# Pooled attention with a feed-forward layer: weight splits on ScalarE and VectorE, and K and V loaded one step sooner

## Chip, core and metric

The kernel runs on one core of one Trainium2 chip. The metric is the device time of one execution in microseconds. Its engines are TensorE (PE, with PEld for its weight loads), VectorE (DVE), ScalarE (ACT), GpSimd (POOL) and SyncE (SP), whose queue issues nearly all DMAs here.

## What is computed

Attention over 4 batches x 8 heads, with the 1152 queries of a head averaged in pairs to 576, and then a feed-forward layer with a residual on the 512-wide result:

```python
q_pool = q.reshape(B, H, S // 2, 2, D).mean(axis=3)          # (4, 8, 576, 64)
scores = matmul(q_pool, k.transpose(0, 1, 3, 2)) / sqrt(D)   # (4, 8, 576, 1152)
attn = exp(scores - max(scores))
attn = attn / (sum(attn) + 1e-09)
x = matmul(attn, v)                                          # heads side by side: (4, 576, 512)
xn = (x - mean(x)) / sqrt(var(x) + 1e-06) * g_ln
out = x + maximum(xn @ w_ch1, 0) @ w_ch2                     # 512 -> 2048 -> 512
```

All inputs and outputs are float32. The kernel keeps float32 accuracy with fp16 matmuls by splitting an operand into a high and a low fp16 part: high = fp16(x), low = fp16(x - high).

## The kernel before

Two heads of a batch make a pair; there are 16 pairs (0 to 15), four for each batch. A pair is worked off in 9 steps of 128 pooled query rows, so there are 144 steps, written here as pair.step or as one number i = 9 x pair + step. The order of all work is written out by hand: `step(i)` issues everything of step i, and each engine runs what it gets in that order.

In step i TensorE computes the scores of step i+1 (`emit_s`, lines 390 and 398) into one of two slots of three PSUM banks. VectorE takes the scores of step i and writes them to SBUF with the row's bound (`emit_max`, line 410), ScalarE makes the exponential (line 417) and its high fp16 part (`emit_hi`, line 428). The low part (`emit_lo`) follows in step i+1: on VectorE (line 437), or, for steps 2, 5 and 8 of a pair, on GpSimd (two instructions, lines 239 and 435). Then SP issues a DMA transpose of both parts (line 440). Four steps after its scores, the product with V runs on TensorE (`emit_pv`, line 480); VectorE and ScalarE evacuate it (lines 528, 529 and 540). The PSUM place of that product lies in the slot that the scores use, so a later step's score matmul of line 398 waits until line 540 has read it. The first batch (steps 0 to 35) does without the DMA transpose and transposes on TensorE in float32.

Besides, each pair needs its inputs. `load` fetches K with two DMAs (lines 117 and 118) and V with one (line 121) into one buffer each, `load_q` fetches q (line 129). `bound` (line 182) reads K, q and V on ScalarE for a bound of their size; from these `scales_reduce`, three steps into the pair before, finds scales over TensorE and VectorE. `prep_k` and `prep_q` transpose K and q on TensorE (lines 285, 289, 312, 321) and split them on ScalarE and VectorE (lines 274 and 271), one unit a step, in the order of the table `PREPS`. `take_v` scales and splits V on GpSimd (lines 239 and 266) in two halves, at steps 5 and 7.

When all heads of a block of rows are done, the block is normalized and its feed-forward work goes into a queue of units: first layer (line 631, evacuated by lines 644 on ScalarE and 645 on VectorE) and second layer (line 663, evacuated by line 677 on VectorE). `some_units` issues one unit in a step, and two once the steps are over; a unit is issued only when the weights it needs are split, which `w_done` counts.

The weights come as four parts of four pieces (n = 0 to 15, each 128 x 1024). A piece is scaled and split into slot n of `wsl` out of slot n+1: `w_split_a` scales in place, `w_split_b` makes the high part, `w_split_c` the low part, all three on GpSimd (lines 239 and 806). `w_splits` plans them: the first two parts one instruction at a time during the first batch, the last two parts at fixed steps, 40 to 58. `at(i, ...)` puts work at the end of step i, `pre(i, ...)` at its start. The loads of pair p and its bounds are planned in one loop, with i0 the first step of pair p-1:

```python
at(max(i0 - 1, 0), load, p, "k", nc.sync)
at(i0, load, p, "v", nc.sync)
at(i0 + 1, bound, p, "k")
...
at(i0 + 2, bound, p, "v")
```

Of the kernel before, what the change touches and what calls it, by code (L numbers as in the profile page):

```python
# [9 lines left out]
FP32 = mybir.dt.float32  # L10
# [3 lines left out]
ACTF = mybir.ActivationFunctionType  # L14
ALU = mybir.AluOpType
# [9 lines left out]
def tile_pooled_attention_moe(  # L25
# [18 lines left out]
    nc = tc.nc  # L44
# [4 lines left out]
    C = S // 128  # L49
    HP = H // 2  # L50
# [29 lines left out]
    wsl = const.tile([128, 17, 2, 1024], FP16, name="wsl")  # L80
    gsb = const.tile([128, KD], FP32, name="gsb")
    gs1 = const.tile([128, 2, KD], FP32, name="gs1")
# [5 lines left out]
    wscl = const.tile([128, 4], FP32, name="wscl")  # L88
# [55 lines left out]
    def kt_of(p):  # L144
        st = state(p)
        if "kt" not in st:
            x = tr_p.tile([128, 2304], FP16, tag="kt", name="kt")
            st["kt"] = x[:, 0:2048].rearrange("p (a h n) -> p a h n", a=2, h=2)
            st["k8"] = x[:, 2048:2304].rearrange("p (h n) -> p h n", h=2)
        return st["kt"]  # L150
# [9 lines left out]
    def pool_q(p, eng):  # L160
        x = raws[p, "q"]
        eng.tensor_tensor(x[:, :, 0], x[:, :, 0], x[:, :, 1], op=ALU.add)

    def dup_q(p, eng):
        x = raws[p, "q"]
        eng.tensor_copy(x[:, :, 1], x[:, :, 0])
# [71 lines left out]
    def scaled(dst, src, s=1.0):  # L238
        nc.gpsimd.tensor_scalar(dst, src, s, 1.0, op0=ALU.mult, op1=ALU.mult)  # L239
# [98 lines left out]
    def prep_q_first():  # L338
# [17 lines left out]
    PREPS = (  # L356
        ((prep_k, 0), (prep_k, 2), (prep_q, 0), (prep_q, 1), (prep_k, 1), (prep_q, 2)),
        ((prep_k, 0), (prep_k, 2), (prep_q, 0), (prep_k, 1), (prep_q, 2), (prep_q, 1)),
    )


# [2 lines left out]
    def on_pe(i):  # L364

        return 0 <= i < HP * C
# [394 lines left out]
    def w_reduce(part):  # L761
        while fill:
            drip()
        x, m = wtop[:, part], wmax[:, part:part + 1]
        nc.vector.tensor_scalar(x, x, 2.0 ** -112, None, op0=ALU.mult)
        xi = x.bitcast(I32)
        nc.vector.tensor_scalar(xi, xi, 3, None, op0=ALU.logical_shift_left)
        if part % 2 == 0:

            nc.vector.tensor_tensor(  # L770
                x, x, gsb[:, :, None].to_broadcast([128, KD, 2]), op=ALU.mult
            )
        nc.vector.tensor_reduce(m, x, axis=AX.XY, op=ALU.max, apply_absolute_value=True)
        reds.extend(all_max(m, 1, lambda ps: (w_scales(part, ps), w_splits(part))))
# [17 lines left out]
    w_done = [0] * 4  # L792

    def w_split_a(n):
        part, c = divmod(n, 4)
        x = wsl[:, n + 1].rearrange("p a n -> p (a n)").bitcast(FP32)
        s = gs1[:, part // 2, c:c + 1] if part % 2 == 0 else wscl[:, part:part + 1]
        scaled(x, x, s)

    def w_split_b(n):  # L800
        x = wsl[:, n + 1].rearrange("p a n -> p (a n)").bitcast(FP32)
# [2 lines left out]
    def w_split_c(n):  # L804
        x = wsl[:, n + 1].rearrange("p a n -> p (a n)").bitcast(FP32)
        nc.gpsimd.tensor_tensor(wsl[:, n, 1], x, wsl[:, n, 0], op=ALU.subtract)
        w_done[n // 4] += 1


    todo = {}  # L810

    def at(i, fn, *a):
        todo.setdefault(i, []).append((fn, a))
# [3 lines left out]
    def pre(i, fn, *a):  # L817
        early.setdefault(i, []).append((fn, a))
# [3 lines left out]

    for p in range(1, NP):
        i0 = (p - 1) * C
        at(max(i0 - 1, 0), load, p, "k", nc.sync)
        at(i0, load, p, "v", nc.sync)
        at(i0 + 1, bound, p, "k")
        if p == 1:
            pre(0, behind_scales)
            pre(i0 + 1, pool_q, p, nc.gpsimd)  # L830
            at(i0 + 1, dup_q, p, nc.gpsimd)
            at(i0 + 2, bound, p, "q")
        elif on_pe(i0):
            at(i0 - 4, load_q, p, (nc.sync,))
            at(i0 - 1, lambda p=p: calm.appendleft((lambda n: pool_q(p, nc.gpsimd), 0)))
            at(i0, lambda p=p: calm.appendleft((lambda n: dup_q(p, nc.gpsimd), 0)))
            at(i0 + 2, bound, p, "q")
        else:
            early_q = not on_pe(i0 - 6)
            at(i0 - (12 if early_q else 8), load_q, p, (nc.sync,))  # L840
            at(i0 - (6 if early_q else 4), pool_q, p, nc.vector)
            at(i0 - 2, bound, p, "q")
            at(i0 - 1, dup_q, p, nc.gpsimd)
        if not on_pe(p * C):
            at(i0 + 2, bound, p, "v")
        pre(i0 + 3, scales_reduce, p, 0, 2 if on_pe(p * C) else 3)
        for n in range(2):
            if on_pe(p * C):
                at(i0 + (5, 7)[n], gate)
            at(i0 + (5, 7)[n], take_v, p, n)  # L850
        for n, (fn, u) in enumerate(PREPS[p % HP // 2]):
            late = 1 if on_pe(i0) else 0
            pre(i0 + 4 + n + late, lambda fn=fn, p=p, u=u: preps.append((fn, p, u)))

# [14 lines left out]
    def w_splits(part):  # L869
        for n in range(4):  # L870
            if part < 2:
                calm.extend((fn, 4 * part + n) for fn in (w_split_a, w_split_b, w_split_c))
                continue
            i0 = 22 + 9 * part + 5 * n // 2
            for x, fn in ((0, w_split_a), (1, w_split_b), (2, w_split_c)):
                at(i0 + x, fn, 4 * part + n)


    norms, fresh, turns = deque(), deque(), set()
# [198 lines left out]
    with tc.manual_schedule():  # L1078
# [15 lines left out]
        for n in (2, 5):  # L1094
# [14 lines left out]
            out=kt_of(0).rearrange("p a h n -> p (a h n)")[:, 0:C * D],  # L1109
            in_=raws[0, "k"][:, 0, 0:C].rearrange("p c d -> p (c d)"), func=ACTF.Abs,  # L1110
# [68 lines left out]
```

## Time and profile before

| | us |
|---|---|
| median of 3 runs (lowest, highest) | 813.52 (812.06, 813.91) |
| the profiled execution's own time | 813.32 |
| its span | 811.50 |
| TensorE busy | 781.8 (96%) |
| VectorE busy | 598.6 (74%) |
| ScalarE busy | 544.0 (67%) |
| GpSimd busy | 342.5 (42%) |

The busy time of TensorE counts each matmul to its modelled end, and matmuls overlap, so a busy TensorE is not one at its peak. Its granted clock is at full speed over nearly the whole span. Steps take from 2 to 8 us between one start of line 410 and the next, about 4.8 in the mean; the last one ends shortly after 690 us. A wait in brackets behind an instruction is the idle time of its engine before it, with what ended it.

### The profile page before, as it was taken

Reading aid. Unit: us, or ns where it says so; the run is one execution under the profiler, and the core shown is the slowest. Engines: PE = TensorE matmul, PEld = TensorE weight load, DVE = VectorE, ACT = ScalarE, POOL = GpSimd, SP = SyncE. Lnnn points to the kernel's source line nnn. Section 1 sums busy time; section 2 is a strip of 40 time slices with the busy share of each in tenths; the row PEclk is TensorE's granted clock in tenths of the full one; section 3 lists DMA queues with packets and bytes.
Section 4 is the critical chain, followed back from the end, with each engine's and each line's share of the span. In section 5 each row is a group of like instructions: output and inputs, shape, how many; then the busy total and the mean of one; then the engine's idle time right before and its main releaser. Section 6 shows DMA issues by size and latency. Waiting matters only on the chain.

```text
span 811.5 us, 21278 instructions
## 1 busy us (share of the span) xinstructions
PE 781.8 (96%) x8936; PEld 551.8 (68%) x8936; DVE 598.6 (74%) x1179; ACT 544.0 (67%) x789; POOL 342.5 (42%) x342
## 2 busy tenths in 40 slices
PE   8999999989989999989999999999999999999997
PEld 6788887767565656567666665767575757766764
DVE  5899999878898986898687877887786867521221
ACT  5889888777767777787677686877677776211010
POOL 2012333576999862665453535537161532300000
PEclk9999999999999999999999999999999999999999
DMA  9736545025998989896989798987979786401001
GB/s 282 241 107 219 192 135 172 2 72 109 168 181 154 179 167 201 164 213 116 202 143 220 147 212 145 186 163 144 197 135 196 131 145 121 86 1 27 14 1 27
DMA packets 276017, 115.95 MB, mean 143 GB/s; under 512 B 259280, under 2 KB 259280, under 8 KB 275920
## 3 DMA queue, kind: packets, MB, share of 16 engines
q1 hardware_dynamic: 275440, 113.63, 67.9%
q8 instruction: 70, 1.15, 0.6%
q10 hardware_dynamic: 480, 0.95, 0.4%
q14 instruction: 27, 0.22, 0.1%
HBM read 46.14 MB, written 4.72 MB: 63 GB/s over the span
## 4 chain that ended last, share of the span: by engine, by line
PE 63%; DVE 16%; ACT 7%; DMA 6%; issue 4%; SPq 2%; POOL 2%; ACTq 0%; DVEq 0%
PE psum L663 19%; PE psum L631 17%; PE psum L390 7%; PE psum L480 6%; PE psum L471 5%; DVE pe L410 5%; PE psum L447 3%; DVE hl L437 3%; DMA vr<-in_v_dram 2%; PE psum L398 2%; ACT pe L417 2%; SPq L440 2%; DMA kr<-in_k_dram 1%; DMA stage<-in_moe_w_ch_dram 1%; PE psum L321 1%
## 5 line engine op out<-in xcount | busy, mean ns | idle before, releaser
L410 DVE CUSTOM_DVE_ANT_0 pe<-psum,nought,sc 128x1152 f32<-128x1152 f32 x144 | 203.0, 1410 | 25.2 <-PE psum L197 9.7
L417 ACT ACTIVATE pe<-pe,nb 128x1152 f32<-128x1152 f32 x144 | 180.4, 1253 | 32.4 <-DVE nb L410 31.2
L663 PE MATMUL psum<-wsl,ht 128*128 128x512 f16 x864 | 196.6, 379 | 2.5 <-DVE ht L645 2.1
L631 PEld LDWEIGHTS <-wsl 128*128 128x128 f16 x1920 | 169.6, 98 | 25.3 <-issue 7.6
L631 PE MATMUL psum<-xn,wsl 128*128 128x256 f16 x1536 | 176.3, 273 | 6.6 <-DVE xb L677 3.8
L663 PEld LDWEIGHTS <-ht 128*128 128x128 f16 x864 | 81.1, 98 | 90.9 <-issue 3.1
L428 ACT ACTIVATE hl<-pe 128x1152 f16<-128x1152 f32 x108 | 125.6, 1163 | 3.4
L390 PE MATMUL psum<-kt,qt 64*128 64x512 f16 (+1 forms) x960 | 120.2, 380 | 1.0 <-ACT qt L274 0.7
L644 ACT ACTIVATE ht<-psum 128x512 f16<-128x512 f32 x72 | 42.7, 593 | 115.4 <-PE psum L631 112.2
L437 DVE SCALAR_TENSOR_TENSOR hl<-pe,hl 128x1152 f16<-128x1152 f32 x72 | 113.3, 1573 | 0.0
L480 PE MATMUL psum<-vt,pt 128*128 128x65 f16 (+2 forms) x3240 | 106.8, 193 | 0.0
L645 DVE SCALAR_TENSOR_TENSOR ht<-psum,ht 128x512 f16<-128x512 f32 x72 | 49.3, 685 | 72.3 <-ACT ht L644 72.3
L480 PEld LDWEIGHTS <-pt 128*128 128x128 f16 (+1 forms) x3240 | 98.4, 100 | 2.6 <-issue 0.2
L239 POOL TENSOR_SCALAR pe<-pe 128x1152 f32<-128x1152 f32 x36 | 41.4, 1149 | 118.8 <-ACT hl L428 118.8
L435 POOL TENSOR_TENSOR hl<-pe,hl 128x1152 f16<-128x1152 f32 x36 | 85.6, 2378 | 3.0
L471 PE MATMUL psum<-pt,vt 128*65 128x128 f32 (+1 forms) x720 | 77.4, 263 | 1.3 <-DVE kt L271 1.3
L471 PEld LDWEIGHTS psum<-pt,vt 128*65 128x65 f32 x720 | 71.5, 138 | 1.5 <-DVE kt L271 1.5
L390 PEld LDWEIGHTS <-qt 64*128 64x128 f16 (+1 forms) x960 | 31.7, 96 | 47.6 <-issue 29.5
L398 PEld LDWEIGHTS <-qt 128*128 128x128 f16 (+1 forms) x320 | 17.6, 99 | 65.8 <-issue 65.6
L677 DVE SCALAR_TENSOR_TENSOR xb<-psum,inv,xb 128x512 f32<-128x512 f32 x32 | 23.8, 744 | 36.3 <-PE psum L663 36.1
L271 DVE SCALAR_TENSOR_TENSOR qt<-psum,s,qt 128x512 f16<-128x512 f32 (+2 forms) x49 | 29.7, 606 | 28.3 <-ACT qt L274 27.9
L453 ACT COPY pt<-psum 128x512 f32<-128x512 f32 x72 | 44.2, 639 | 7.1 <-PE psum L447 6.0
(116 smaller groups left out, 939.9 us busy)
## 6 DMA issues: line engine op xcount, KB each, us to landing
stage<-in_moe_w_ch_dram SPq DMA_DIRECT2D x32, 512.0 KB, 6.2
kr<-in_k_dram SPq DMA_DIRECT2D x16, 576.0 KB, 4.7
vr<-in_v_dram SPq DMA_DIRECT2D x16, 576.0 KB, 5.0
qr<-in_q_dram SPq DMA_DIRECT2D x31, 288.0 KB, 4.8
out_dram<-xb SPq DMA_DIRECT2D x28, 128.0 KB, 3.0
pt<-hl SPq DMA_TRANSPOSE x108, 4.9
kr<-in_k_dram SPq DMA_DIRECT2D x16, 64.0 KB, 4.5
out_dram<-xb ACTq DMA_DIRECT2D x4, 128.0 KB, 2.6
```

The costliest lines, as they stand in the source:

```text
L390: nc.tensor.matmul(out=sp[o:o + w, c0:c0 + 512], lhsT=qt[r:r + 64, qa, q0:q0 + w], rhs=kt[r:r + 64, ka, h], start=(a == 0), stop=(a == 2),)
L410: nc.vector.tensor_tensor_reduce(out=st["pe"], in0=st["s"], in1=nought[:, 0:1].to_broadcast([128, S]), scale=pair[i // C]["sc"][:, 0:1], s ...
L417: nc.scalar.activation(out=st["pe"], in_=st["pe"], func=ACTF.Exp, scale=-1.0, bias=st["nb"])
L428: nc.scalar.activation(out=hl[:, 0], in_=st["pe"], func=ACTF.Copy, scale=2.0 ** 15)
L435: nc.gpsimd.tensor_tensor(hl[:, 1], st["pe"], hl[:, 0], op=ALU.subtract)
L437: nc.vector.scalar_tensor_tensor(hl[:, 1], st["pe"], 2.0 ** 15, hl[:, 0], op0=ALU.mult, op1=ALU.subtract)
L453: nc.scalar.copy(st["pt"][:, a:b], st["s"][:, a:b])
L471: nc.tensor.matmul(out=ps[0:65, q0:q0 + w], lhsT=vt[:, h, c], rhs=pt[:, 128 * u + q0:128 * u + q0 + w], start=(u == 0), stop=(u == C - 1),)
L480: nc.tensor.matmul(out=dst[:, 0:n], lhsT=pt[:, a + u, q0:q0 + w], rhs=vt[:, h, c, x0:x0 + n], start=(u == 0 and a == 0 and n == 65), stop= ...
L631: nc.tensor.matmul(out=ps[:, o:o + n], lhsT=wsl[:, 8 * w + cc, wa, f * 128:f * 128 + 128], rhs=xn[:, xa * KD + cc, 0:n], start=(m == 0), s ...
L645: lambda: nc.vector.scalar_tensor_tensor(lo, pv, 0.0, hi, op0=ALU.max, op1=ALU.subtract),
L663: nc.tensor.matmul(out=ps, lhsT=hv[0][:, ha, f, t * 128:t * 128 + 128], rhs=wsl[:, 8 * w + 4 + f // 2, wa, (f % 2) * DM:(f % 2) * DM + DM] ...
```

## The change

Three things are changed.

The splits of the last two weight parts leave GpSimd. For each piece ScalarE writes the high part with the scale in the same instruction (`w_split_hi`), and one step later VectorE writes the low part from the unscaled piece, the scale and the high part (`w_split_lo`). There are eight such pieces; the high parts stand at the ends of steps 38, 41, 44, 47, 50, 53, 56 and 59, the low parts one step after. The in-place scaling is gone.

From pair 6 on (`i0 > 36`), K is loaded at the end of step i0 - 2 instead of i0 - 1, V at i0 - 1 instead of i0, and the bound of K is issued at i0 instead of i0 + 1. The bound of V and everything behind it stay.

Since K has one buffer, the old K must be transposed before the new one may land. A third order in `PREPS` puts the second half of K ahead of the second part of q; it holds for pairs 5, 8, 9, 12 and 13.

```diff
     PREPS = (
         ((prep_k, 0), (prep_k, 2), (prep_q, 0), (prep_q, 1), (prep_k, 1), (prep_q, 2)),
         ((prep_k, 0), (prep_k, 2), (prep_q, 0), (prep_k, 1), (prep_q, 2), (prep_q, 1)),
+        ((prep_k, 0), (prep_k, 2), (prep_q, 0), (prep_k, 1), (prep_q, 1), (prep_q, 2)),
     )
...
     def w_split_a(n):
-        part, c = divmod(n, 4)
         x = wsl[:, n + 1].rearrange("p a n -> p (a n)").bitcast(FP32)
-        s = gs1[:, part // 2, c:c + 1] if part % 2 == 0 else wscl[:, part:part + 1]
-        scaled(x, x, s)
+        scaled(x, x, w_scale(n))
...
+    def w_scale(n):
+        part, c = divmod(n, 4)
+        return gs1[:, part // 2, c:c + 1] if part % 2 == 0 else wscl[:, part:part + 1]
+
+    def w_split_hi(n):
+        x = wsl[:, n + 1].rearrange("p a n -> p (a n)").bitcast(FP32)
+        nc.scalar.activation(out=wsl[:, n, 0], in_=x, func=ACTF.Copy, scale=w_scale(n))
+
+    def w_split_lo(n):
+        x = wsl[:, n + 1].rearrange("p a n -> p (a n)").bitcast(FP32)
+        nc.vector.scalar_tensor_tensor(
+            wsl[:, n, 1], x, w_scale(n), wsl[:, n, 0], op0=ALU.mult, op1=ALU.subtract
+        )
+        w_done[n // 4] += 1
...
         i0 = (p - 1) * C
-        at(max(i0 - 1, 0), load, p, "k", nc.sync)
-        at(i0, load, p, "v", nc.sync)
-        at(i0 + 1, bound, p, "k")
+
+        ahead = 1 if i0 > HP * C else 0
+        at(max(i0 - 1 - ahead, 0), load, p, "k", nc.sync)
+        at(i0 - ahead, load, p, "v", nc.sync)
+        at(i0 + 1 - ahead, bound, p, "k")
...
-        for n, (fn, u) in enumerate(PREPS[p % HP // 2]):
+        for n, (fn, u) in enumerate(PREPS[p % HP // 2 or (0 if on_pe(i0) else 2)]):
...
-            i0 = 22 + 9 * part + 5 * n // 2
-            for x, fn in ((0, w_split_a), (1, w_split_b), (2, w_split_c)):
-                at(i0 + x, fn, 4 * part + n)
+
+            i0 = 12 * part + 3 * n + 14
+            at(i0, w_split_hi, 4 * part + n)
+            at(i0 + 1, w_split_lo, 4 * part + n)
```

## Rows read from the trace of the kernel before

**Rows 1.** Stretches: engines' busy us (instructions), TensorE's clock, DMA share, GB/s.
```profile
171.70:300.90 129.20, 121.19 (x1492) 82.25 (x1491) 113.12 (x185) 97.73 (x133) 107.50 (x79) 1.00 0.81 155
...
690.00:811.50 121.50, 117.22 (x976) 80.12 (x972) 32.15 (x57) 16.32 (x31) 6.02 (x14) 1.00 0.12 26
```

**Rows 2.** TensorE's waits, 171.7 to 300.9 us: total us, times, longest.
```profile
PE psum L631 <- DVE xb L677: 3.0, 2, 1.6
PE psum L631 <- DVE ht L645: 1.8, 4, 0.8
```

**Rows 3.** The same from 300.9 to 690 us.
```profile
PE psum L398 <- ACT xb L540: 4.4, 5, 1.6
```

**Rows 4.** Timeline of pair 5, all engines: start, us, engine, line, operation, tiles.
```profile
221.23 2.38 POOL L435 TENSOR_TENSOR hl<-pe,hl 128x1152 f16<-128x1152 f32 x1
221.58 3.25 DVE L437 SCALAR_TENSOR_TENSOR hl<-pe,hl 128x1152 f16<-128x1152 f32 x1
...
226.41 0.73 DVE L677 SCALAR_TENSOR_TENSOR xb<-psum,inv,xb 128x512 f32<-128x512 f32 x1
...
227.19 2.78 PE L631 MATMUL psum<-xn,wsl 128*128 128x256 f16 x24 [1.60 <-DVE xb L677]
```

**Rows 5.** VectorE's line 437, 171.7 to 300.9, then 429.3 to 560.7: busy, mean ns.
```profile
L437 DVE SCALAR_TENSOR_TENSOR hl<-pe,hl 128x1152 f16<-128x1152 f32 x18 | 36.5, 2028 | 0.0
...
L437 DVE SCALAR_TENSOR_TENSOR hl<-pe,hl 128x1152 f16<-128x1152 f32 x19 | 27.1, 1426 | 0.0
```

**Rows 6.** Timeline of SP's queue, 296 to 313 us, with the issue's duration.
```profile
296.82 4.08 SPq L440 DMA_TRANSPOSE pt<-hl  x1
...
302.33 2.78 SPq L440 DMA_TRANSPOSE pt<-hl  x1
305.21 0.52 SPq L117 DMA_DIRECT2D kr<-in_k_dram  x1
...
306.38 5.48 SPq L440 DMA_TRANSPOSE pt<-hl  x1
311.90 0.58 SPq L121 DMA_DIRECT2D vr<-in_v_dram  x1
```

**Rows 7.** Timeline of ScalarE, 300 to 319 us, with waits.
```profile
304.86 0.63 ACT L540 ACTIVATE xh<-psum,r 64x64 f32<-64x64 f32 x2
...
311.71 1.16 ACT L182 ACTIVATE kt<-kr 128x1152 f16<-128x1152 f32 x1 [2.40 <-DMA kr<-in_k_dram]
...
316.63 1.16 ACT L182 ACTIVATE kt<-vr 128x1152 f16<-128x1152 f32 x1 [1.12 <-DMA vr<-in_v_dram]
```

**Rows 8.** Timeline of TensorE, 296 to 322 us.
```profile
297.61 0.60 PE L285 MATMUL psum<-ident,kr 128*128 128x128 f32 x4
...
310.37 0.98 PE L480 MATMUL psum<-vt,pt 128*128 128x65 f16 x27
...
315.56 0.30 PE L398 MATMUL psum<-kt,qt 128*64 128x128 f16 x4 [0.82 <-ACT xb L540]
```

**Rows 9.** ScalarE's waits for DMAs, 171 to 690 us: total, times, longest.
```profile
ACT kt L182 <- DMA vr<-in_v_dram: 10.4, 8, 2.6
ACT kt L182 <- DMA kr<-in_k_dram: 8.2, 4, 3.4
```

**Rows 10.** ScalarE by line and shape, 259 to 300.9 us.
```profile
L428 ACT ACTIVATE hl<-pe 128x1152 f16<-128x1152 f32 x9 | 10.5, 1163 | 0.3
```

**Rows 11.** Timeline of ScalarE in pair 13, 560 to 577 us.
```profile
565.79 0.63 ACT L540 ACTIVATE xh<-psum,r 64x64 f32<-64x64 f32 x2
...
574.04 1.16 ACT L182 ACTIVATE kt<-kr 128x1152 f16<-128x1152 f32 x1 [3.41 <-DMA kr<-in_k_dram]
```

**Rows 12.** Line 440: issue to landing of the transposes issued at 302.33 and 306.38.
```profile
DMA to landing us min/median/max: 4.7/4.7/4.7
...
DMA to landing us min/median/max: 7.6/7.6/7.6
```

**Rows 13.** Timeline of GpSimd, 286 to 300 us: the last use of V.
```profile
294.23 1.25 POOL L266 TENSOR_TENSOR vt<-vr,vt 128x576 f16<-128x576 f32 x1
```

## The prediction

> **What bounds the kernel now.** I read the stretches first. From 690 us on, after the last scores, TensorE alone works through the feed-forward units that are left: 117.2 of 121.5 us busy [rows 1]. What it does there is fixed, so any microsecond in which TensorE stands still earlier is added to the end, and any that is saved comes off. The question for every edit is thus only how long TensorE waits, and for whom. Between 171.7 and 300.9 us, where the weights' last two parts are split, GpSimd is busy 107.5 of 129.2 us and VectorE 113.1 [rows 1]. I then read TensorE's waits in that stretch: 3.0 us in two waits of a layer-one unit (line 631) for VectorE's evacuation of a result (line 677), and 1.8 us in four for line 645 [rows 2]. Behind it, from 300.9 to 690, the largest named wait is that of the score matmuls (line 398) for ScalarE's line 540: 4.4 us in five [rows 3]. Little more than these is there to win: 4.8 us in the first stretch, 4.4 in the second.
>
> The timeline shows how the first wait arises. GpSimd's low part (line 435) starts at 221.23 and takes 2.38, to 223.61; VectorE's low part (line 437) starts at 221.58 and takes 3.25, to 224.83, that is 1.22 after GpSimd ended; the evacuation then comes at 226.41 and line 631 starts at 227.19, 1.60 late [rows 4]. On GpSimd, whose order is that of the code, weight splits stand between its low parts in this stretch, which fills it. Line 437 takes 2.03 us in the mean of this stretch and 1.43 in a later one without splits [rows 5].
>
> The second wait starts on the SP queue. In pair 8 (pairs and steps counted from 0) the load of K is issued at 305.21, the transpose behind it occupies SP for 5.48, and only at 311.90 comes the load of V [rows 6]. ScalarE, which takes its work in order, stands 2.40 us before the bound of K and 1.12 before that of V [rows 7], and the score matmul at 315.56 waits 0.82 for what ScalarE does behind them [rows 8]. Over the run these are 10.4 us for V in eight waits and 8.2 for K in four [rows 9]; only part reaches TensorE, the 4.4 us above.
>
> **The change part by part.** *The splits leave GpSimd.* Eight splits of three instructions each go; GpSimd is no bound, so this alone is worth nothing. What it gives is that the low parts of steps 44 and 53 no longer stand behind a split, so line 437 and the evacuation behind it come in time: I take both waits of rows 2 as gone, -3.0. The 1.8 us for line 645 I leave, since that line waits on ScalarE as well. Bounds: 0 if VectorE is late for another reason, -4.8 if all of rows 2 goes.
>
> *Eight ScalarE instructions of 128x1024 are added*, at the ends of steps 38, 41, 44, 47, 50, 53, 56 and 59. The nearest row is line 428, 1.163 us for 1152 columns [rows 10], so 1.03 scaled to 1024 and 1.16 at most: 8.3 to 9.3 us in all, of which TensorE sees nothing as long as ScalarE has idle time in the step. At steps 47 and 56 the instruction stands right behind the bound of V; there it takes the place of a wait for V of over two microseconds in this stretch's pairs. Without that cover each instruction could hold the line 540 behind it by 1.1 us, so the bound is 0 to +9; I take 0, by rows 2, which name no wait for line 540. The first, at step 38, must wait until GpSimd has read the last part-one weight; the bound of V stands before it on ScalarE, so I take 0 here too, and 1 us as the other end.
>
> *Eight VectorE instructions of 128x1024 are added*, one step behind each. By line 437's 1.43 us at 1152 columns, 1.27 each, 10.1 us in all. They fall on steps 39, 42, 45, ..., 60, whose predecessor gives its low part to GpSimd, so VectorE issues no line 437 there: the load is evened out. Against it stand 18 x (2.03 - 1.43) = 10.8 us that line 437 loses [rows 5]. VectorE's sum is unchanged; I take 0 for TensorE, with -1 to +4 as bounds. The last part becomes ready at step 60 rather than 58; by the order of the code the unit that needs it all stands in step 61 in either version, so no unit moves.
>
> Here a row speaks against the change. The VectorE instruction of rows 4 ended 1.22 us after GpSimd's, as if it had not begun until then, and the new one also reads two tiles from SBUF while GpSimd does its low part of the same step. The Trainium skill ("SBUF — State Buffer", section "Who interferes with whom") says that a VectorE instruction with two SBUF inputs contends with a GpSimd instruction that reads SBUF; by that rule, with which the row agrees, each new instruction can be held as line 437 was. What this would do is the second rival below.
>
> *K's and V's loads move one step up, from pair 6 on.* K's load is two DMAs, V's one; all stay on SP. K now passes one transpose (that of the pair's step 7, which follows it instead of leading it), V passes that of step 8. In pair 8 K would be issued when the transpose of 296.82 has ended, at 300.90, 4.3 us sooner; the next transpose takes the 5.48 that the one behind K took, so V follows at about 303.4 + 5.5 = 309, 3 us sooner [rows 6]. V's bound stays where it is, and V then lands some 4.7 later at 313.7, before ScalarE asks at 315.5: the waits for V go. K's bound moves up with K, so its wait stays, changed by ScalarE's step less SP's time between the two places. Pair 8: ScalarE is free at 305.49 instead of 309.31, 3.8 us; SP gains 4.3; the wait falls from 2.4 to 1.9 [rows 6, 7]. Where no store stands between, SP gains only one transpose, 2.8 [rows 6]: in pair 14 ScalarE is free at 566.42 rather than 570.63, so 3.41 becomes 4.8 [rows 11]. By their share of the waits (10.4 of 18.6) V's are worth 2.5 of the 4.4 us; K's in the pairs like 14 cost back 0.9.
>
> The queue pays for it. The transpose behind the load of K landed 7.6 us after its issue, the one ahead of it 4.7 [rows 12]. That of step 7 now stands behind K: issued 1.1 later and 2.9 longer on its way, it lands 4.0 us later, in pair 8 at 311.0 instead of 307.0, and its product starts at 310.37 [rows 8]: 0.6 us late. Step 8's, now behind V too, lands by my estimate 2.7 later (that 2.9 less what a place further up saves), at 316.7, some 0.8 behind its product, which follows the matmul of 315.56. These two are one delay, not two, since TensorE takes them in order. I count it in the three or so pairs in which SP runs this tightly, less what TensorE has lost there already: +0.8. Loads in sum: -2.5 + 0.9 + 0.8 = -0.8, bounds -4.4 and +8.
>
> The two waits that move cost nothing by their rows: K's load needs the last transposes of the old K, which TensorE ends at 298.21 in pair 7 [rows 8], before SP gets to it at 300.9; V's needs GpSimd's last use of the old V, over at 295.48 [rows 13]. Behind either wait stand all further transposes. Two preparations of K and q swap places in some pairs to make that so; the instructions are the same, 0.
>
> **Rivals.** *Transposes late (slower).* If SP is as tight in all ten pairs 6 to 15, the transpose of step 7 decides from the point where its landing moves by more than the 3.4 us that lie between 307.0 and 310.37. Ten times 0.8 is +8, and with V's gain unseen and the splits' -3.0 that is +5: 818.5. For it: the rows of pair 8. Against it: after the fourth transpose of a pair SP is waiting for its input again, so some pairs have more room.
>
> *The lock eats the splits' gain (no change).* Each new VectorE instruction may stand behind a 2.38 us low part of GpSimd [rows 4]: up to 8 x 2.4 = 19 us more on VectorE, late enough to bring the two waits of rows 2 back. Then only -0.8 is left: 812.7. Against it: those steps have no line 437, so VectorE has room in them.
>
> *All waits go.* TensorE's 4.8 and 4.4 us [rows 2, 3] both vanish: 804.3. Against it: K's wait stays by the working above.
>
> **How the numbers follow.** The profiled run took 813.3 us, 811.5 of it span; the median of the runs shown is 813.5, 0.2 above. -3.0 - 0.8 = -3.8 from 813.3 gives 809.5, and set against the median 809.7. Chances: forecast 0.52 (806 to 812.5), lock 0.17, transposes late 0.18, all waits go 0.08, something else 0.05. The range goes from 804.0 to 815.5 and leaves out most of the late transposes (0.14) and a little of the rest. A measurement of this kernel can tell about 0.2% (1.6 us) from no change. Faster by more: 0.46 of the forecast, 0.08 of the last rival, 0.03 of the lock and 0.04 of the rest: 0.61. Within: 0.05 and 0.13: 0.18. Slower: 0.18 and a few hundredths: 0.21.
>
> **What would show it.** After: line 437 near 1.4 us between 200 and 300 us and no wait of line 631 for line 677 there; no wait of ScalarE for V, but one for K of 1 to 5 us, largest in pairs 10 and 14; transposes of steps 7 and 8 landing 3 to 4 us later in their step, with TensorE's product (line 480) waiting for them under a microsecond in a few pairs. The prediction is wrong if TensorE waits for transposes in most pairs, or if VectorE stays at or above its 113 us in the first stretch and its evacuations stay late.

## The result and the profile after

The change makes the kernel slower: 823.14 us in the median of 4 runs (820.78 to 824.73) against 813.18 (812.06 to 813.91) of the kernel before beside it, a ratio of 1.0108 with a 95% interval of 1.0088 to 1.0128. The profiled execution took 824.37 us, 822.4 of it span; before's took 813.32 and 811.5. From the table `PREPS` on, most lines that this document names stand one higher than before: 398 is 399, 410 is 411, 437 is 438, 480 is 481, 540 is 541, 645 is 646. New are line 815 (ScalarE's half of a split) and line 819 (VectorE's).

**Where the time went.** The length of a pair is read from the start of line 410 (411) in its first step to that of the next pair. Below, "A late bound" is the changed kernel with the bound of K back at its old step, and "again" is a second profiled execution of the changed kernel; both are experiments further down.

| pair | before | after | after, again | splits alone | loads alone | A late bound |
|---|---|---|---|---|---|---|
| 4 | 44.64 | 45.79 | 45.79 | 45.78 | 44.64 | 45.77 |
| 5 | 42.77 | 42.21 | 42.22 | 42.00 | 42.94 | 41.99 |
| 6 | 41.80 | 42.25 | 42.50 | 42.30 | 42.30 | 41.99 |
| 7 | 44.15 | 43.18 | 43.19 | 44.25 | 43.45 | 42.35 |
| 8 | 41.13 | 41.31 | 41.32 | 40.96 | 41.31 | 40.98 |
| **9** | 43.15 | **49.34** | 47.41 | 43.18 | 49.07 | 42.78 |
| 10 | 42.62 | 42.63 | 42.62 | 42.62 | 42.62 | 43.85 |
| **13** | 44.10 | **47.34** | 45.90 | 43.04 | 47.14 | 43.04 |

K and V of a pair are loaded around the start of the pair before it, so what happens to K of pair 10 shows in pair 9 of the table, and K of pair 14 in pair 13.

Pairs 11, 12, 14 and 15 differ by less than 0.1 between before and after. (In the second execution pair 11 is 0.8 longer too, with a wait of 1.39 us for K.) The profiled execution of after loses 6.2 us in pair 9 and 3.2 in pair 13; pairs 4 to 8 together lose 0.2, and 1.2 us arise before pair 4, where the code is the same. That is 10.8 of the span's 10.9. The 1.2 us go with 3.4 us at half of TensorE's clock, from 14.2 us on, which the trace of before does not have; the last section shows that this differs between executions whatever the kernel. Behind the steps TensorE works as it did [rows 1].

The first view is that of stretches: busy us (instructions) of PE, PEld, DVE, ACT and POOL, then the granted clock, DMA share and GB/s.

```profile
14.00:18.00 4.00, 3.17 (x26) 2.54 (x25) 1.43 (x4) 1.75 (x3) 2.07 (x2) 0.57 1.04 346
174.10:303.70 129.60, 121.14 (x1486) 81.50 (x1484) 114.84 (x193) 105.39 (x141) 65.07 (x55) 1.00 0.84 158
...
397.00:400.00 3.00, 2.96 (x19) 1.55 (x20) 2.45 (x4) 1.80 (x3) 0.00 (x0) 0.50 0.91 264
400.00:403.00 3.00, 3.00 (x30) 1.87 (x28) 2.27 (x4) 1.37 (x3) 0.00 (x0) 0.50 1.24 153
579.00:582.00 3.00, 2.26 (x16) 1.84 (x16) 3.00 (x4) 2.73 (x4) 0.00 (x0) 0.81 0.99 223
582.00:585.00 3.00, 3.00 (x20) 1.50 (x19) 1.18 (x5) 0.96 (x2) 0.00 (x0) 0.63 1.13 237
700.00:822.40 122.40, 118.05 (x982) 80.86 (x980) 32.16 (x57) 16.32 (x31) 6.85 (x14) 1.00 0.12 26
```

GpSimd is relieved in the stretch of the splits (65.1 us, from 107.5), and VectorE is hardly busier than it was (114.8, from 113.1). Three spells at the half clock, 1.2 instead of 2.4 GHz, are in this trace: the one at 14 us, one in pair 9 and one in pair 13. Before's first stretch reads:

```profile
14.00:18.00 4.00, 3.52 (x42) 2.79 (x42) 2.35 (x6) 2.36 (x3) 2.77 (x4) 1.00 1.04 315
```

The waits of after come next (total us, times, longest): TensorE's from 171.7 to 303 us, which answer to [rows 2], then its largest from 303 to 700, to [rows 3], then ScalarE's only one for a load, to [rows 9].

```profile
PE psum L632 <- DVE ht L646: 2.0, 4, 1.1
PE psum L664 <- DVE ht L646: 1.7, 2, 0.8
...
PE psum L632 <- DVE xb L678: 1.1, 2, 0.7
PE psum L587 <- DVE qt L271: 1.0, 1, 1.0
PE psum L321 <- DVE ht L646: 0.9, 1, 0.9
...
PE psum L632 <- DVE ht L646: 4.2, 4, 3.2
PE psum L587 <- DVE qt L271: 4.1, 2, 3.6
...
PE psum L399 <- ACT xb L541: 1.2, 2, 1.0
...
ACT kt L182 <- DMA kr<-in_k_dram: 5.7, 3, 3.1
```

The waits of the score matmul for line 541 fell from 4.4 to 1.2 us, and no wait for V is left. Two others came that before did not have: 3.6 us in one piece before line 587 (a transpose of the normalized block) and 3.2 before line 632 (a first-layer unit). The timeline shows how they arise, first in pair 9, then in pair 13; its last four lines are those of the loads of pair 8, for [rows 6, 7].

```profile
390.08 0.59 SPq L117 DMA_DIRECT2D kr<-in_k_dram  x1
...
390.66 2.75 PE L664 MATMUL psum<-wsl,ht 128*128 128x512 f16 x12
...
391.87 0.61 ACT L541 ACTIVATE xh<-psum,r 64x64 f32<-64x64 f32 x2
394.86 1.16 ACT L182 ACTIVATE kt<-kr 128x1152 f16<-128x1152 f32 x1 [2.38 <-DMA kr<-in_k_dram]
...
396.14 0.37 ACT L274 ACTIVATE qt<-psum,s 128x128 f16<-128x128 f32 x1
396.54 0.35 DVE L271 SCALAR_TENSOR_TENSOR qt<-psum,s,qt 128x128 f16<-128x128 f32 x1 [5.41 <-ACT qt L274]
...
397.04 1.08 PE L587 MATMUL psum<-ident,xs 128*128 128x128 f32 x4 [3.62 <-DVE qt L271]
...
398.06 1.46 PE L391 MATMUL psum<-kt,qt 64*128 64x512 f16 x6
...
399.64 1.68 PE L481 MATMUL psum<-vt,pt 128*128 128x65 f16 x27
...
572.45 0.53 SPq L117 DMA_DIRECT2D kr<-in_k_dram  x1
...
574.71 0.82 PE L391 MATMUL psum<-kt,qt 64*128 64x512 f16 x6
...
577.08 1.16 ACT L182 ACTIVATE kt<-kr 128x1152 f16<-128x1152 f32 x1 [3.06 <-DMA kr<-in_k_dram]
...
578.36 0.60 ACT L645 ACTIVATE ht<-psum 128x512 f16<-128x512 f32 x1
...
578.99 0.69 DVE L646 SCALAR_TENSOR_TENSOR ht<-psum,ht 128x512 f16<-128x512 f32 x1 [5.15 <-ACT ht L645]
...
579.74 4.26 PE L632 MATMUL psum<-xn,wsl 128*128 128x256 f16 x24 [3.17 <-DVE ht L646]
...
302.53 0.58 SPq L117 DMA_DIRECT2D kr<-in_k_dram  x1
...
307.72 1.16 ACT L182 ACTIVATE kt<-kr 128x1152 f16<-128x1152 f32 x1
...
309.10 0.52 SPq L121 DMA_DIRECT2D vr<-in_v_dram  x1
...
315.67 1.15 ACT L182 ACTIVATE kt<-vr 128x1152 f16<-128x1152 f32 x1
```

In pair 9 SP issues the load of K at 390.08. ScalarE is free at 392.5 and stands 2.38 us before the bound of K. Behind that bound in its order is the high part of the last unit of q (line 274), whose low part VectorE makes (line 271), and only then may TensorE write the same PSUM place with line 587. All three engines stand in one row behind one load: VectorE 5.41 us, TensorE 3.62. Then the clock is at half, and the six matmuls of line 391 take 1.46 us where the same six take 0.82 at 574.71. Pair 13 is the same with a first-layer unit: K, bound, line 645, line 646, line 632, whose 24 matmuls take 4.26 us for 2.78 [rows 4]. K of pair 8 is there when ScalarE asks.

### The profile page after: what moved, and what is told of

Its sections match the earlier page's. It is cut to its first block, busy times and chain, and to the rows that moved or that the text cites. A ratio compares the mean times of both kernels' runs of the same rounds, so it can differ in the third digit from the quotient of the medians.

```text
span 822.4 us, 21276 instructions
## 1 busy us (share of the span) xinstructions
PE 786.7 (96%) x8936; PEld 553.7 (67%) x8936; DVE 600.5 (73%) x1187; ACT 553.2 (67%) x797; POOL 300.8 (37%) x318
## 4 chain that ended last, share of the span: by engine, by line
PE 69%; DVE 15%; ACT 9%; issue 4%; DMA 3%; POOL 0%; SPq 0%; DVEq 0%; ACTq 0%; POOLq 0%
PE psum L632 20%; PE psum L664 19%; PE psum L391 8%; PE psum L481 7%; PE psum L472 5%; DVE pe L411 5%; PE psum L448 3%; PE psum L399 2%; ACT pe L418 2%; DMA kr<-in_k_dram 2%; DVE hl L438 2%; PE psum L321 1%; DVE ht L646 1%; ACT kt L182 1%; ACT hl L429 1%
## 5 line engine op out<-in xcount | busy, mean ns | idle before, releaser
L481 PE MATMUL psum<-vt,pt 128*128 128x65 f16 (+2 forms) x3240 | 107.5, 194 | 0.0
L438 DVE SCALAR_TENSOR_TENSOR hl<-pe,hl 128x1152 f16<-128x1152 f32 x72 | 102.9, 1430 | 0.0
L239 POOL TENSOR_SCALAR vt<-vr,s 128x576 f16<-128x576 f32 x24 | 23.2, 967 | 74.0 <-DVE e L232 74.0
```

The lines of the kernel that those rows point to most:

```text
L438: nc.vector.scalar_tensor_tensor(hl[:, 1], st["pe"], 2.0 ** 15, hl[:, 0], op0=ALU.mult, op1=ALU.subtract)
L481: nc.tensor.matmul(out=dst[:, 0:n], lhsT=pt[:, a + u, q0:q0 + w], rhs=vt[:, h, c, x0:x0 + n], start=(u == 0 and a == 0 and n == 65), stop= ...
```

## The experiments

Three theories were to be told apart. **A**: the bound of K, one step further up, puts its wait for the load in front of evacuations that TensorE needs next. **B**: the transposes, now behind K and V on SP, come late. **C**: the splits on ScalarE and VectorE hold their other work up. Each diff is against the changed kernel unless it says otherwise.

**Splits alone** (`e1_split_only`): loads, bound and `PREPS` as before.

```diff
-        at(max(i0 - 1 - ahead, 0), load, p, "k", nc.sync)
-        at(i0 - ahead, load, p, "v", nc.sync)
-        at(i0 + 1 - ahead, bound, p, "k")
+        at(max(i0 - 1, 0), load, p, "k", nc.sync)
+        at(i0, load, p, "v", nc.sync)
+        at(i0 + 1, bound, p, "k")
```

> The changed kernel with the loads, the bound of K and the order of the preparations put back: only the splits are on ScalarE and VectorE. Theory A (the bound of K, moved one step up on ScalarE, waits for K in front of evacuations that TensorE needs): the loss is not here, 812.5 to 815.5; in the changed kernel's trace the stretch of the splits ends about 1 us later than it began, against the kernel before. Theory C (the loss is ScalarE's and VectorE's new work): 818 or more. My prediction had put the splits at -3 us, which would be 810.

Measured: 814.78 us (10 runs) against 814.44, a ratio of 0.9999 (0.9984 to 1.0014). The splits are worth nothing, and they cost nothing, to within 1.2 us either way; C is not the loss.

**Loads alone** (`e2_loads_only`): the splits back on GpSimd.

```diff
-            i0 = 12 * part + 3 * n + 14
-            at(i0, w_split_hi, 4 * part + n)
-            at(i0 + 1, w_split_lo, 4 * part + n)
+            i0 = 22 + 9 * part + 5 * n // 2
+            for x, fn in ((0, w_split_a), (1, w_split_b), (2, w_split_c)):
+                at(i0 + x, fn, 4 * part + n)
```

> The kernel before with the loads, the bound of K and the preparations' order of the changed one; the splits stay on GpSimd. Theory A: about the changed kernel's time, 819 to 824, with pairs 9 and 13 several microseconds longer than before. Theory C: about the kernel before, 811 to 815. Theory B (transposes come late behind the loads): 819 to 824 too, but spread over most pairs.

Measured: 824.05 us (4 runs), 1.0117 (1.0092 to 1.0142). The whole loss is here, with the same two waits of TensorE and the same pairs 9 and 13.

**The bound of K at its old step** (`e3_bound_k_late`): all else as changed, the loads sooner too.

```diff
-        at(i0 + 1 - ahead, bound, p, "k")
+        at(i0 + 1, bound, p, "k")
```

> The changed kernel with only the bound of K put back to the step it had; K and V are still loaded a step sooner. Theory A: the loss goes, ScalarE no longer waits for K or V, and pairs 9 and 13 are as long as before or shorter: 809 to 814. Theory B: the transposes are as late as in the changed kernel, so 819 to 823 stays.

Measured: 812.35 us (6 runs), 0.9963 (0.9940 to 0.9987), that is faster than before. One line moved by one step turns a loss of 1.1% into a gain of 0.4%. ScalarE waits for neither K nor V, pairs 9 and 13 are at 42.78 and 43.04, and TensorE's waits from 303 to 700 us read:

```profile
PE psum L208 <- DVE diag L201: 2.2, 2, 1.1
PE psum L481 <- DMA pt<-hl: 1.8, 3, 1.2
...
PE psum L399 <- ACT xb L541: 0.7, 1, 0.7
```

The late transposes of B are real, 1.8 us in three waits, and pair 10 is 1.2 longer than before. They are seen with V alone sooner as well (2.0 in three waits), and in all such traces they are far from 10 us. A holds, B does not.

**Pairs 10 and 14 left as before** (`e4_not_10_14`), all others one step sooner.

```diff
-        ahead = 1 if i0 > HP * C else 0
+        ahead = 1 if i0 > HP * C and p not in (10, 14) else 0
```

> The changed kernel, but the inputs of pairs 10 and 14 are loaded and bound as before; the other eight pairs from 6 on keep the new places. Theory A: ScalarE's waits for K go back to 1.8 and 3.4 us where they were harmless, so 812 to 815. Theory B: a loss spread over ten pairs shrinks by two tenths only, 819 to 822.

Measured: 815.17 us (10 runs), 1.0015 (1.0000 to 1.0030); pair 9 42.79, pair 13 44.62. The loads of two pairs out of ten carry nearly all of the loss.

**V alone one step sooner** (`e5_v_only`), K, its bound and `PREPS` as before (the diff leaves the line of `PREPS` out), splits as changed.

```diff
-        at(max(i0 - 1 - ahead, 0), load, p, "k", nc.sync)
+        at(max(i0 - 1, 0), load, p, "k", nc.sync)
         at(i0 - ahead, load, p, "v", nc.sync)
-        at(i0 + 1 - ahead, bound, p, "k")
+        at(i0 + 1, bound, p, "k")
```

> The changed kernel with K's load, K's bound and the preparations' order as before; only V is loaded one step sooner, so that it follows K directly. Theory A: ScalarE's waits for V go, those for K stay where they were harmless; 811 to 814.5, a little behind the run with K and V early and the bound late, since ScalarE still waits for K. If an early V made the transposes late, 815 or more.

Measured: 814.24 us (10 runs), 1.0004 (0.9986 to 1.0022). No wait for V is left in any pair, yet no gain can be told; the wait for K of pair 14 stays, with 2.36 us, and TensorE waits three times for a transpose.

**q two steps sooner** (`e8_q_sooner`): in the changed kernel SP issues a load of q some 6 us ahead of the late loads of K (at 384.44 with K at 390.08, at 565.33 with K at 572.45). This edit takes q away from there and leaves the bound at its new place.

```diff
-            at(i0 - (12 if early_q else 8), load_q, p, (nc.sync,))
+            at(i0 - (14 if early_q else 8), load_q, p, (nc.sync,))
```

> The changed kernel with q's loads two steps sooner, so that they no longer stand on SP right ahead of K's; the bound of K stays at its new place. Theory A in the form that ScalarE's wait for K does the harm: K lands some 3 us sooner in pairs 10 and 14, the waits of 2.4 and 3.1 us fall below 0.5, time 812 to 816. In the form that the place of the bound's own 1.35 us of work ahead of the evacuations does it: 819 to 823.

Measured: 815.50 us (10 runs), 1.0014 (0.9999 to 1.0030); pairs 9 and 13 at 44.08 and 43.67. ScalarE's waits for loads from 303 to 700 us are down to one:

```profile
ACT kt L182 <- DMA kr<-in_k_dram: 1.1, 1, 1.1
```

So the wait for K does most of the harm, not the 1.35 us of work that the bound puts in front of the evacuations. The one wait that is left is in pair 13. In pair 9 ScalarE no longer waits for K, line 587 still waits 1.27 us, and the 0.9 that the pair loses stay with the place.

**Bound late and q sooner** (`e9_bound_late_q_sooner`): the edits of the third and the last experiment together.

> The bound of K at its old step, K and V early, and q two steps sooner. By theory A nothing on ScalarE waits for a load any more, and the transposes of steps 6 to 8 have more room: the products' waits for transposes (1.8 us in three with the bound late alone) go, 808 to 812. If q is not what crowds SP there, as with the bound late alone, 810 to 814.

Measured: 810.02 us (5 runs) against 813.97, 0.9958 (0.9944 to 0.9972); no wait of TensorE for a transpose, pair 10 at 42.62, pair 13 at 42.36. It beats both kernels. Against the bound late alone, on another chip, the ratio is not distinguishable; the pairs are 1.2 and 0.7 us shorter.

**The same with pieces 8 and 9 on GpSimd** (`e10_first_two_on_gpsimd`), to win back the 1.1 us of pair 4, **and with all splits as before** (`e11_e9_old_splits`). The diff shows what the first adds to the run above.

```diff
+            if part == 2 and n < 2:
+                for x, fn in ((0, w_split_a), (1, w_split_b), (2, w_split_c)):
+                    at(38 + 2 * n + x, fn, 4 * part + n)
+                continue
```

> As the run with the bound late and q sooner, but the first two of the eight pieces are split on GpSimd as in the kernel before, two steps earlier than there. If the 1.1 us that pair 4 got longer come from the first two instructions on ScalarE and VectorE (in front of evacuations of steps 39 and 42), pair 4 goes back to 44.6 us and the time falls by about 1 to 808 to 810. If they come from elsewhere, 809.5 to 811.

> As the run with the bound late and q sooner, but all splits on GpSimd as in the kernel before. If moving the splits is worth nothing by itself, as the run with only the splits moved says (ratio 0.9999), about the same time, 809 to 811.5. If the splits' place only pays once the loads come early, 811.5 to 813.5; my prediction's -3 us for the splits would show here.

Measured: 810.81 us (5 runs), 0.9952 (0.9934 to 0.9970), and 810.88 (6 runs), 0.9954 (0.9939 to 0.9969). Pair 4 is at 46.15 in the first, so giving the first two pieces back to GpSimd does not win its loss back, and at 44.63 in the second. Where the splits run makes no difference that can be told; the gain over before comes from the order of the loads.

**Matmuls in the gaps.** Is the half clock part of the loss, or does it only accompany it? 55 matmuls that nothing reads were put ahead of the two waits: `e7_matmuls_in_gap` with both groups in the step's third PSUM bank, `e12_gap_other_bank` with the second group in its first bank. The diff is that of the latter.

```diff
+    def in_gap(i, n, b, c):
+        for _ in range(n):
+            nc.tensor.matmul(
+                out=psum[:, 3 * (i % 2) + b, c:c + 125], lhsT=ident16, rhs=ident16[:, 0:125], start=True, stop=True
+            )
...
+            if i == 118:
+                in_gap(i, 55, 0, 0)
             some_units(i)
...
+        if i == 81:
+            in_gap(i, 55, 2, 387)
         for fn, a in todo.pop(i, ()):
```

> The changed kernel with 55 small matmuls in front of TensorE's long wait in each of steps 81 and 118 (some 3 us each, into PSUM columns that nothing reads; they add work that the result does not use). The waits themselves stay. If part of the loss is the lowered TensorE clock behind these waits (6.8 and 3.4 us at half clock in the changed kernel), the clock stays up there and the time falls to 817.5 to 821. If the clock only goes with the waits and costs nothing of its own, 822 to 825.

> The changed kernel with 55 matmuls of 128x125, which nothing reads, ahead of TensorE's two waits of 3.6 and 3.2 us, the second group now in a PSUM bank that no engine still reads. The waits themselves stay, only TensorE is busy in them. If the half clock is a cost of its own, behind the waits: no half clock in pairs 9 and 13, pair 9 at 45.7 us (49.3 in the changed kernel), pair 13 at 45.6 (47.3, less half of the 3.4 us at half clock), the time 817 to 819.5, ratio about 1.006 to the kernel before. If the half clock costs nothing of its own: pairs as in the changed kernel, 822 to 824. If it were all of the loss: pairs 9 and 13 at 43.2 and 44.1, 813 to 814.

The first took 826.54 us (4 runs), 1.0168 (1.0142 to 1.0194), and missed: in pair 9 the matmuls filled the gap (45.74 us, no half clock), but in pair 13 they had themselves to wait 4.89 us for line 541, which still had to read their bank, and the pair took 52.01, with 3.4 us at the half clock in it. The second shows both gaps filled; its TensorE in pair 9:

```profile
391.80 3.19 PE L1006 MATMUL psum<-ident 128*128 128x125 f16 x55
395.33 0.63 PE L587 MATMUL psum<-ident,xs 128*128 128x128 f32 x4 [0.34 <-DVE qt L271]
```

The granted clock is at full speed throughout, pairs 9 and 13 are at 46.13 and 46.18, and the profiled execution took 818.57 us, as expected. The median did not follow: 821.53 (4 runs), 1.0110 (1.0091 to 1.0129). So both kernels were run once more, beside each other on one chip.

> The changed kernel once more, beside the one with matmuls in its two gaps and on the same chip, to size the half clock's share of the loss by times and not by the pairs of one execution. Both theories: 1.009 to 1.013 of the kernel before, half clock in pairs 9 and 13.

> The kernel with 55 idle matmuls ahead of each of the two waits once more. If the half clock costs what the pairs of the profiled execution say (3.2 and 1.2 us): 4 to 5 us less than the changed kernel beside it, 1.004 to 1.007 of the kernel before. If it is worth no more than the 1.6 us between the medians so far: 0 to 2 us less, 1.009 to 1.012, and then the waits themselves are most of the loss in most executions.

Measured: 821.85 us (6 runs), 1.0108 (1.0086 to 1.0130), for the changed kernel; 821.04 (6 runs), 1.0098 (1.0080 to 1.0116), with the matmuls. That is 0.8 us, the second of the two answers written down. The changed kernel's second trace tells why: TensorE around the two waits, and then the clock (busy us of PE, clock, DMA share, GB/s).

```profile
395.64 1.09 PE L587 MATMUL psum<-ident,xs 128*128 128x128 f32 x4 [3.20 <-DVE qt L271]
...
577.91 2.78 PE L632 MATMUL psum<-xn,wsl 128*128 128x256 f16 x24 [3.38 <-DVE ht L646]
```

```profile
394.00:396.00 2.00, 0.36 (x2) 0.84 1.25 185
396.00:398.00 2.00, 2.00 (x10) 0.50 0.82 276
398.00:400.00 2.00, 2.00 (x35) 0.80 2.01 217
...
576.00:578.00 2.00, 0.09 (x1) 1.00 1.09 199
578.00:580.00 2.00, 2.00 (x20) 1.00 1.09 283
```

The waits are there as in the first execution, but the half clock lasts some 3.4 us in pair 9 where it lasted 6.8, and does not come in pair 13 at all: the 24 matmuls behind a wait of 3.38 us take their usual 2.78. The half clock is thus an addition that differs from execution to execution. Pair 9 costs 2.6 to 3.0 us with its gap filled (45.74, 46.13 and 46.05 in three executions, against 43.15) and 4.3 to 6.2 with it open; pair 13 costs 2.1 and 2.6 with its gap filled, 1.8 with the gap open and no half clock, 3.2 with one. Each of these is uncertain by up to 1 us: pair 13 takes 44.10 in the trace of before and 43.04 with the splits alone, whose loads are the same.

In the medians of these last two kernels the half clock is some 1 us of the loss, with an uncertainty of about its own size, and the waits are most of the rest: with both gaps filled, pairs 9 and 13 together lose 5.1 us in the first trace, as much as its span loses, and 5.5 of 6.9 in the second. The medians lose 8.6 and 8.1. The slower executions were not traced, so the other 3 us are not placed. The mean granted clock is on record for every execution, and says that the half clock has no fixed price: it is 0.992 to 0.995 in the first four executions of the changed kernel, 0.992 to 0.998 in these six, 0.995 to 1.000 in the six with the matmuls beside them and 0.996 to 1.000 in the eleven of before. By my estimate (twice what is missing to 1, times the span of 820 us) that is 8 to 13 us at half clock in the first four and 0 to 8 with the matmuls. So some spells lie elsewhere than behind the two waits, and by this estimate the half clock cost more than 1 us in the first four executions.

## Why the prediction was wrong

The prediction said 809.7 us with 0.61 for faster. The kernel is at 823, outside the range and on the other side.

**The step that failed** is "K's in the pairs like 14 cost back 0.9". The wait itself was foreseen: one of ScalarE for K of 1 to 5 us, largest in pairs 10 and 14. It was 2.4 and 3.1, even under the 4.8 worked out for pair 14. What was wrong is its price. The working gave K's wait the price that waits of ScalarE have in [rows 3], through line 398, as if the bound had stayed where it was. But the bound moved, and what stands behind it on ScalarE moved with it: at its new place that is line 274 of q's last unit or line 645, both of which release TensorE's very next instruction. So a wait of 2.4 us for K, with the bound's own 1.35 behind it, became one of 3.6 for TensorE, and one of 3.1 became 3.2: at least the whole wait arrived, where the share had let a quarter through (4.4 of 18.6). The sentence on ScalarE's order was in the prediction for the splits ("right behind the bound of V") and missing for the bound that the change moves. Restoring that one line (812.35) shows it. The +0.9 itself has no working: for pair 14 alone, 1.4 us more at that share is 0.33. The term of +0.9 measures some 5 us without the half clock (pairs 9 and 13 of the kernel with the gaps filled) and 9.4 in the first profiled execution.

**The clock** was not in the sum at all. From 171.7 us on no wait of before was longer than 1.6 us [rows 2, 3], and its clock is at full speed over the stretches read [rows 1], so there was no row to price it from; it is a miss of some 1 us in the medians of the last pair of runs, of some 4 in pairs 9 and 13 of the first profiled execution (9.4 less 5.1 to 5.5), and of 1.2 more at its start, which differs between executions of the same code.

**The splits' -3.0** measured 0. The two waits for line 677 shrank from 3.0 to 1.1 us, as the step said, and line 437 came to 1.4 us in that stretch, as forecast. But VectorE stayed above 113 us there, with 114.8, half of one of the prediction's signs of being wrong, and other waits grew. Of these, before had the following two beside [rows 2]:

```profile
PE psum L663 <- DVE ht L645: 0.9, 2, 0.5
...
PE psum L321 <- DVE ht L645: 0.4, 1, 0.4
```

After they are 1.7 and 0.9, line 587's wait for line 271 is new with 1.0, and the wait for line 645 (646) went from 1.8 to 2.0: +2.5 against -1.9, less 0.2 at line 398 (399), and the stretch is 0.4 longer (129.6 for 129.2). The timeline shows one of them, at step 50:

```profile
247.28 1.14 ACT L815 ACTIVATE wsl<-wsl,wscl 128x1024 f16<-128x1024 f32 x1
248.32 0.58 ACT L645 ACTIVATE ht<-psum 128x512 f16<-128x512 f32 x1
...
248.94 0.69 DVE L646 SCALAR_TENSOR_TENSOR ht<-psum,ht 128x512 f16<-128x512 f32 x1 [0.28 <-ACT ht L645]
...
249.30 2.37 POOL L436 TENSOR_TENSOR hl<-pe,hl 128x1152 f16<-128x1152 f32 x1
...
249.68 2.75 PE L664 MATMUL psum<-wsl,ht 128*128 128x512 f16 x12 [0.85 <-DVE ht L646]
...
250.18 2.57 DVE L819 SCALAR_TENSOR_TENSOR wsl<-wsl,wscl 128x1024 f16<-128x1024 f32 x1
```

ScalarE's split stands between lines 541 and 645, and its 1.14 us reach TensorE as 0.85 at line 664. The eight ScalarE instructions were taken as 0 because no row named a wait for line 540; the evacuation that they hold is line 645's, a row that the prediction had read and left aside. The bound of 0 to +9 held it, the chosen value did not. What makes the rest of pair 4's 1.1 us was not separated.

**The lock** was rightly a rival. Of the eight instructions of line 819, three overlap no low part of GpSimd and take 1.27 us, as priced; the other five do, take 2.23 to 2.87, and end 1.07 to 1.09 us after GpSimd's instruction (here 252.75 behind 251.67). The rule of the Trainium skill ("SBUF — State Buffer", section "Who interferes with whom") agrees with the trace in all eight. The hold adds 6.4 us to VectorE (12.8 less 5 x 1.27), about a third of the 19 that bounded it. Line 437 loses what was worked out, 11.1 us for 10.8:

```profile
L438 DVE SCALAR_TENSOR_TENSOR hl<-pe,hl 128x1152 f16<-128x1152 f32 x18 | 25.4, 1409 | 0.0
...
L819 DVE SCALAR_TENSOR_TENSOR wsl<-wsl,wscl 128x1024 f16<-128x1024 f32 x4 | 9.3, 2321 | 0.1
L819 DVE SCALAR_TENSOR_TENSOR wsl<-wsl,gs 128x1024 f16<-128x1024 f32 x4 | 7.3, 1829 | 0.0
```

It reaches TensorE in one place that the trace shows: the instruction of 206.77 takes 2.55 us, line 271 follows at 209.68, and line 587 starts 1.02 late. So the rival's result (the splits give nothing) came true, in part by its mechanism and in part by ScalarE's.

**V's waits** went in every pair, as forecast, and line 399's with them, from 4.4 to 1.2 us. By itself this gained nothing that can be told (1.0004 for V alone). **Late transposes** cost +0.8 in the sum; in after TensorE has no wait for them, and with the bound late they are 1.8 in three waits. Their rival had the right sign for a reason that did not occur. **The wait for K of pair 8**, worked out as 1.9, is not there: SP reached the load of K at 302.53 and ScalarE asked at 307.7, 5.2 later.

The sum as it came out, for the profiled execution: splits 0 instead of -3.0, K +9.4 instead of +0.9, transposes 0 instead of +0.8, and 1.2 us at the start that were not in the sum. Of the -2.5 for V, pair 7 shows 1.0 (43.18 for 44.15), and other pairs take it back: pairs 4 to 8 together are 0.2 longer. No run shows the rest.

## What to carry to other kernels

When an instruction that waits for a load is moved on an engine that works in order, price the wait anew at the new place: write down the next three instructions behind it and ask which of them TensorE needs for its next step. Here the loads moved up by themselves did no harm (812.35 us); their first reader moved up with them kept the wait and changed whom it held. And an instruction given to an engine with idle time is not free as long as it stands ahead of an evacuation.

## What the runs showed of the hardware

A wait of TensorE of 3 to 4 us was followed by a spell at 1.2 GHz in some executions and not in others: 6.8 us of it behind a wait of 3.62, 3.4 behind one of 3.20, 3.4 behind one of 3.17 and none behind one of 3.38. Each us at the half clock takes about half a us from the matmuls in it (24 matmuls behind the wait of 3.17 take 4.26 us instead of 2.78). The length of the wait alone did not decide, and what does stays open.

A spell can also come 14 to 16 us into the execution, where the code of all these kernels is the same, and where they stand later goes with it. Seven of the fifteen traces, before's among them, have none there, and their pair 2 starts at 90.2 to 90.7 us; five, after's first among them, have 3.4 us of it and start pair 2 at 91.7 to 92.1; three have 6.8 us and start it at 92.8 to 92.9. So pairs were compared, not places in the span.

The wait for K of pair 14 differed between executions of the same order of loads: 2.70 to 4.06 us in the six traces that have it at the new place.
